# A prologue worked chunk by chunk, and a new order of all tasks, in a delta-rule attention with a routed expert layer

## The chip, the core and the metric

The kernel runs on one NeuronCore of a Trainium2 chip. The core has a matrix engine (TensorE, PE in the profile), a vector engine (VectorE, DVE), a scalar engine (ScalarE, ACT), a general engine (GpSimd, POOL) and a synchronising engine (SyncE, SP) which here only issues transfers. Each engine works through its own queue in order. Transfers between HBM and the on-chip memory SBUF are issued from the queues of SP, ACT and POOL, and the products of TensorE land in a separate memory, PSUM. The metric is the device time of one execution in microseconds (us), as the median of several runs.

## The reference

Two blocks follow one another. The first is a delta-rule attention over 4 batches of 8 heads, 768 steps and 48 features. With normalised keys, each step reads the state and then corrects it:

```python
for t in range(S):
    kt, vt, bt = (k_n[:, :, t], v[:, :, t], beta[:, :, t, None])
    y[:, :, t] = np.einsum('bhd,bhde->bhe', q[:, :, t], state)
    v_old = np.einsum('bhde,bhd->bhe', state, kt)
    state = state + bt[:, :, :, None] * np.einsum('bhd,bhe->bhde', kt, vt - v_old)
```

The second block takes the 3072 tokens of 384 features that come out. It chooses for each token one of 8 experts by the largest cosine with an expert's embedding, and computes `gate * (relu(x @ w1[e]) @ w2[e])` with that expert's weights (384x1024 and 1024x384). The gate is the softmax probability of the chosen expert.

## The kernel before

**Attention in chunks.** The 768 steps are cut into 12 chunks of `C = 64` steps (index m). Two batches and two heads stand side by side in the 128 rows of a tile. A chunk is worked in two *units* (n = 2m and 2m + 1, one for each pair of batches), so there are 24 units. Inside a chunk the steps are not taken one by one: the corrections of the 64 steps solve a triangular system, whose matrix comes from the products of the keys with one another, and the kernel forms inverses of its two 32x32 diagonal blocks once for each *group* g of two chunks (four units). There are 6 groups.

**From keys to inverses (`prepare(g)`).** For each chunk: load the keys k in eight transfers, two halves i with four each (`planned_k`, `load_swapped`, L283). Square them on ScalarE (L440), sum on VectorE (L445), take the root and its reciprocal and scale by the root of beta (L464, L389 to L391, L471, L479), and multiply the keys (L497). Turn them on TensorE (L298) and copy them out of PSUM on ScalarE into `KQ`. Multiply the keys with one another (`gram_keys`) and bring the diagonal blocks of both chunks into `stage`. One 128x1024 transpose on VectorE (L569) lays the blocks of all heads into lanes; POOL masks the upper part (`lower`, L574); and VectorE eliminates column by column, a product (L585 or L601) and a subtraction (L590 or L605) for each column.

**The first group is special.** For group 0 (`FINE`) the elimination runs only in two 16x16 blocks, columns 1 to 14 of 16, and TensorE finishes the 32x32 inverses: the row part goes back from the lanes (`rows_from_lanes`, L615) and is copied into `W` (`rows_spread`, two copies on ScalarE), then the rest (`from_lanes`, L620). Then come 64 small products (`level_one`), a copy to SBUF on ScalarE (`level_one_out`), 64 more products (`level_two`), a merge on VectorE (`merged`, L652) and two copies of the inverses into `W` on ScalarE (`spread`). A fp32 product stands in the trace as two records. The other groups eliminate all 30 columns on VectorE and have only the two copies at the end.

**A unit.** `gram` multiplies keys with keys and queries; `corner` (ScalarE, into `Sx`) and `scores` (VectorE, into `M`) mask the results. Then comes the chain: the product of state and keys (`old`), its subtraction from the scaled values V (`rest`, L758, into R), `solve` with W, copy Y, `fix`, copy U, `solve_again`, copy Z, `update`, and the new state on VectorE (L807; L809 in the first chunk). The first two units have no state, and begin with `solve`. `inside` and `from_state` give the unit's outputs, which go to the tokens' tile, are turned, and give the router's logits. `routing` works groups of four units: it writes tokens and lists of their numbers by expert to HBM (L1048, L1054).

**The order.** All of the attention stage is a list of tasks with dependencies (`plan.add`). The table `ORDER` gives the one order in which `Plan.emit` issues them. So each engine's queue is fixed by the table, and a task that waits holds up everything behind it on its engine. The numbers for busy time and due time in `plan.add` do not act at run time. Where two engines read one tile of PSUM, the second also waits for the first.

**Constants and loads.** `start_constants` fills zero columns on POOL, `masks` makes the masks on VectorE and fills `Sx` and `W` on POOL. Beta is loaded first on SP. Key halves go through SP, but the second half of chunk 0 through ScalarE's queue and that of chunk 1 through POOL's. `late_constants4` (L939 to L950) makes token numbers on VectorE.

**The experts.** Behind the plan, from L1312 on, tiles of up to 256 tokens are gathered and multiplied with the weights of their expert (L1278 and L1295). Weights of expert 0 are loaded into `w1_first` and `w2_first` during attention, in space that keys and inverses no longer use; two tiles of expert 0 are computed early.

## Time and profile before

| what | value |
|---|---|
| time, median of 3 runs | 603.27 us (599.58 to 604.70) |
| the profiled execution's own time | 605.27 us |
| its span, first to last instruction | 603.5 us |
| mean granted TensorE clock | 0.904 |
| TensorE busy | 520.3 us (86%) |
| VectorE busy | 275.3 us (46%) |
| ScalarE busy | 202.8 us (34%) |
| GpSimd busy | 171.9 us (28%) |
| first square of keys starts | 10.39 us |
| first solve of a unit starts | 74.60 us |
| first product of the experts' stage starts | 334.62 us |
| transfers | 90.49 MB |

A line of the timeline gives the start in us from the span's start, the length in us, the engine, the line of the code, the operation, and what it writes and reads ("out<-in") with the tile's size; "x2" means that neighbours are merged. Square brackets give the idle time ahead of it and what ended that. A line of windows gives the stretch and its length, the busy time of TensorE's products, its weight loads, VectorE, ScalarE and GpSimd (each with the number of instructions), the granted clock, the busy share of the transfer engines and GB/s. Names of tiles can be those of the space in which they lie: the keys lie in `w1_first`, and lanes and inverses in `w2_first`, which both read `w_first`.

### The profile page before, as it was taken

The page shows a single profiled execution, that of the slowest core. Times are in us where ns is not written, and L with a number is a line of the kernel's source. Part 1 is how long each engine was busy: PE and PEld are TensorE (multiplying, and loading weights), DVE is VectorE, ACT ScalarE, POOL GpSimd, SP SyncE. Part 2 cuts the span into 40 slices and gives each one's busy share as a digit, 9 for nine tenths or more (in the row PEclk, how much of TensorE's full clock was granted, in tenths as well). Part 3 has the DMA queues.
Part 4 walks back from the last instruction along what each step waited for, and adds up shares of the span by engine and source line. Part 5 has one row for each costly group of instructions (what it writes and reads, how often), then busy time and mean ns, then how long its engine had stood idle before and what let it go on. Part 6 is the DMA issues. An engine that isn't in the chain of part 4 may idle for free. (4 is left out here: it accounts for less than half of the span.)

```text
span 603.5 us, 20901 instructions
## 1 busy us (share of the span) xinstructions
PE 520.3 (86%) x9131; PEld 432.2 (72%) x9131; DVE 275.3 (46%) x756; ACT 202.8 (34%) x378; POOL 171.9 (28%) x230
## 2 busy tenths in 40 slices
PE   4478688987978986898899898999999999999990
PEld 3467587876867885787796777777776877777870
DVE  3796989988777868785315020110011221121100
ACT  2353368565555654437341111101101221110100
POOL 7321662155315305312414013411221111111000
PEclk9875589997697998768899899999999999999996
DMA  3434434355164430005502899997456756789300
GB/s 69 75 69 80 83 69 74 66 96 120 26 183 89 121 99 5 6 4 158 168 18 91 314 383 386 360 376 253 160 158 222 243 160 227 239 257 328 127 17 17
DMA packets 116330, 90.49 MB, mean 150 GB/s; under 512 B 83394, under 2 KB 105308, under 8 KB 116226
## 3 DMA queue, kind: packets, MB, share of 16 engines
q1 hardware_dynamic: 110722, 77.76, 43.8%
q0 software_dynamic: 4416, 11.06, 5.3%
q8 instruction: 76, 1.25, 0.8%
q10 hardware_dynamic: 1088, 0.20, 0.2%
q14 instruction: 28, 0.23, 0.1%
HBM read 77.06 MB, written 12.13 MB: 148 GB/s over the span
## 5 line engine op out<-in xcount | busy, mean ns | idle before, releaser
L1280 ACT ACTIVATE hT<-acc 128x512 f32<-128x512 f32 (+3 forms) x52 | 28.5, 548 | 168.5 <-PE acc L1278 168.4
L1278 PEld LDWEIGHTS acc<-xTm,w 128*128 128x128 f32 x576 | 77.7, 191 | 5.8 <-issue 1.8
L1278 PE MATMUL acc<-xTm,w 128*128 128x128 f32 (+3 forms) x576 | 80.3, 299 | 0.0
L1295 PE MATMUL acc<-w,hT 128*128 128x384 f32 (+2 forms) x272 | 78.9, 489 | 0.0
L1308 POOL DMA_INDIRECT out_dram<-y,more_ids x22 | 21.7, 987 | 160.9 <-DVE y L1298 128.3
L1295 PEld LDWEIGHTS acc<-w,hT 128*128 128x128 f32 (+2 forms) x272 | 42.2, 176 | 30.3 <-issue 5.8
L1269 DVE COPY xTm<-acc 128x384 f32<-128x384 f32 (+3 forms) x26 | 12.7, 509 | 105.6 <-PE acc L1268 104.8
L601 DVE TENSOR_TENSOR tmp<-w_first 128x30 f32<-128x30 f32 (+9 forms) x150 | 57.5, 383 | 4.9 <-POOL w_first L574 0.9
L605 DVE TENSOR_TENSOR w_first<-w_first,tmp 128x30 f32<-128x30 f32 (+9 forms) x150 | 55.9, 373 | 4.2
L1298 DVE TENSOR_SCALAR y<-acc,xg 128x384 f32<-128x384 f32 x20 | 12.4, 618 | 97.7 <-PE acc L1295 93.1
L262 PE MATMUL psum_pair<-KQ 48*64 48x64 f32 (+1 forms) x1536 | 41.4, 260 | 11.3 <-ACT KQ L265 8.2
L1278 PEld LDWEIGHTS acc<-xTm,w_first 128*128 128x128 f32 x288 | 43.7, 196 | 4.1 <-DVE xTm L1269 0.9
L1278 PE MATMUL acc<-xTm,w_first 128*128 128x128 f32 (+3 forms) x288 | 45.9, 321 | 0.8 <-DVE xTm L1269 0.8
L262 PEld LDWEIGHTS psum_pair<-KQ 48*64 48x64 f32 x1536 | 35.6, 156 | 14.7 <-ACT KQ L265 9.4
L1295 PE MATMUL acc<-w_first,hT 128*128 128x384 f32 (+2 forms) x176 | 44.2, 489 | 0.0
L262 PE MATMUL psum_pair<-S,KQ 48*64 48x64 f32 x1408 | 35.3, 247 | 9.1 <-ACT KQ L265 2.2
L262 PEld LDWEIGHTS psum_pair<-S,KQ 48*64 48x64 f32 x1408 | 30.3, 158 | 12.4 <-issue 3.0
L1054 POOL DMA_INDIRECT idmap<-tokid,slots_i x24 | 24.2, 1007 | 47.4 <-DVE tmp L601 20.6
L1295 PEld LDWEIGHTS acc<-w_first,hT 128*128 128x128 f32 (+2 forms) x176 | 23.1, 163 | 17.8 <-issue 4.5
L460 POOL TENSOR_TENSOR rt<-rn,half 128x32 f32<-128x32 f32 x4 | 21.9, 5483 | 32.4 <-DVE rn L445 32.4
L497 POOL TENSOR_TENSOR K<-w_first,rt 128x384 f32<-128x384 f32 x22 | 18.6, 865 | 36.7 <-PE psum_pair L262 18.3
L298 PE MATMUL psum_pair<-ident,K 128*128 128x128 f32 x96 | 18.2, 361 | 12.1 <-POOL space L915 7.1
(225 smaller groups left out, 840.3 us busy)
## 6 DMA issues: line engine op xcount, KB each, us to landing
w<-in_moe_w_dram SPq DMA_DIRECT2D x24, 1536.0 KB, 11.5
w_first<-in_moe_w_dram SPq DMA_DIRECT2D x10, 1536.0 KB, 8.4
q<-in_q_dram SPq DMA_DIRECT2D x96, 48.0 KB, 2.8
v<-in_v_dram SPq DMA_DIRECT2D x48, 96.0 KB, 2.7
w_first<-in_k_dram SPq DMA_DIRECT2D x88, 48.0 KB, 2.4
x_dram<-XC SPq DMA_DIRECT2D x5, 800.0 KB, 5.0
idmap<-space SPq DMA_DIRECT2D x1, 2048.0 KB
w_first<-in_moe_w_dram SPq DMA_DIRECT2D x6, 256.0 KB, 2.9
```

The lines of the kernel that those rows point to most:

```text
L262: nc.tensor.matmul(out_, lhsT=lhsT, rhs=rhs, start=start, stop=True, skip_group_check=True)
L298: nc.tensor.transpose(p[:, i, j * 128:(j + 1) * 128], two, ident)
L460: nc.gpsimd.tensor_tensor(out=flat(rt, part), in0=flat(ss, part), in1=half[:, 0:w], op=ALU.pow)
L497: (nc.vector if m == 1 else nc.gpsimd).tensor_tensor(heads(buf("K", m))[:, i], buf("k", m)[:, i], rt[:, m % 2, i].rearrange("p j jj -> p ( ...
L601: nc.vector.tensor_tensor(t, X[:, j + 1:, j:j + 1].broadcast_to([128, rows, j]), X[:, j:j + 1, 0:j].broadcast_to([128, rows, j]), op=ALU.mult)
L605: nc.vector.tensor_tensor(X[:, j + 1:, 0:j], X[:, j + 1:, 0:j], t, op=ALU.subtract)
L1054: put = nc.gpsimd.indirect_dma_start(out=idmap[:, :], out_offset=bass.IndirectOffsetOnAxis(ap=slot_i[:, i:i + 1], axis=0), in_=K["tokid"][ ...
L1269: nc.vector.tensor_copy(t.xT[:, :, b * T:b * T + n], psX[:, :, 0:n])
L1278: nc.tensor.matmul(psH[:, i, :], lhsT=t.w1[:, j, (f + i) * 128:(f + i + 1) * 128], rhs=t.xT[:, j, 0:t.width], start=(j == 0), stop=(j == K ...
L1280: nc.scalar.activation(t.hT[:, f:f + k, 0:t.width], psH, ACT.Relu)
L1295: nc.tensor.matmul(psO[c:c + w, :], lhsT=t.hT[:, f, b * T + o:b * T + o + w], rhs=t.w2[:, f, :], start=(f < q), stop=(f >= NF - q))
L1308: nc.gpsimd.indirect_dma_start(out=out[:, :], out_offset=bass.IndirectOffsetOnAxis(ap=t.ids[b][0:n, 1:2], axis=0), in_=y[0:n, :], in_offse ...
```

## The change

- **Loads.** The first halves of the keys of chunks 0 to 3 go through SP, the second halves through ScalarE's queue (16 transfers there instead of 4, none on POOL). The queries of chunk 0 (8 transfers) go through POOL's queue.
- **Masks.** `masks` keeps the six small column masks. The wide ones, the fine mask and POOL's fills go to a second task, `more_masks`.
- **Level products.** `level_one`, its copy, `level_two` and `merged` are each made for one chunk's heads (a = 0 or 1) at a time, in one bank of PSUM for each chunk, so that a step of one chunk waits only for that chunk's part. The merge is two instructions for each chunk.
- **Copies of the inverses.** For group 0 they are made for each chunk by itself, in two instructions each; the second block's copies (also that of the row part) are on VectorE instead of ScalarE. A unit reads only its own chunk's part of W.
- **Order.** `ORDER` has 1275 tasks instead of 1270 and is new throughout.

```diff
-            e, name, busy = (nc.sync, "SP", 2.2) if m > 1 or not i else (nc.scalar, "ACT", 2.8) if m == 0 else (nc.gpsimd, "POOL", 4.0)
+            e, name, busy = (nc.sync, "SP", 2.2) if m > 3 or not i else (nc.scalar, "ACT", 2.1)
...
+            plan.add("DVE", 2.0, 0.2, -39.0, more_masks, reads=["iotas", "masks"], writes=["masks2"])
...
                 def rows_spread(b=b, name=name):
-                    act_copy(W[:, :, b * HC:b * HC + LC], WN.rearrange("p r x -> p x r"), K[name])
+                    o, i_ = W[:, :, b * HC:b * HC + LC], WN.rearrange("p r x -> p x r")
+                    if b:
+                        nc.vector.tensor_scalar_mul(o, i_, K[name])
+                    else:
+                        act_copy(o, i_, K[name])
...
+            def level_one(a):
                 def step():
                     p = pair(level)
-                    for x in xs:
+                    for x_, x in enumerate(half_x[a]):
                         for o in range(2):
-                            mm(p[HALF[o], 0, x * LC:(x + 1) * LC], W[HALF[o], x], WT[HALF[o], LC:, x])
+                            mm(p[HALF[o], a, x_ * LC:(x_ + 1) * LC], W[HALF[o], x], WT[HALF[o], LC:, x])
...
+            def level_one_out(a):
+                to = WN.rearrange("p r x -> p (r x)")[:, a * HX:(a + 1) * HX]
+                return lambda: act_copy(to, pair(level)[:, a, 0:HX], K["lo"])
...
+            def merged(a):
+                def step():
+                    p = pair(level)[:, a, HX:2 * HX].rearrange("p (jj n c) -> p jj n c", jj=2, c=LC)
+                    for jj in range(2):
+                        to = WT.rearrange("p c (jj m n) -> p jj m n c", jj=2, m=2)[:, jj, a, :, LC:]
+                        nc.vector.scalar_tensor_tensor(out=to, in0=p[:, jj], scalar=K["lo"], in1=to, op0=ALU.mult, op1=ALU.add)
+                return step
...
+            if g == 0:
+                for a in range(2):
+                    def spread(b=b, name=name, a=a):
+                        for jj in range(2):
+                            x0 = jj * 16 + a * 8
+                            o, i_ = W[:, x0:x0 + 8, b * HC:(b + 1) * HC], WT.rearrange("p i x -> p x i")[:, x0:x0 + 8]
+                            if b:
+                                nc.vector.tensor_scalar_mul(o, i_, K[name])
+                            else:
+                                act_copy(o, i_, K[name])
...
-                load_swapped(nc.sync, by_head(heads(buf("q", m))), q, m, i)
+                load_swapped(nc.sync if m else nc.gpsimd, by_head(heads(buf("q", m))), q, m, i)
...
-        W_, S_ = [at("W", n // 4) + (0,), at("W", n // 4) + (1,)], ("S", i)
+        W_, S_ = [at("W", n // 4) + (b, m % 2) for b in range(2)], ("S", i)
```

## The prediction

> **What bounds the kernel now.** I read the page's slices first, then the timeline of the first 95 us, then the later timeline of VectorE, then windows with the granted clock. The slices show two stages: an attention stage, in which no engine is full, up to about 320 us, and an expert stage in which TensorE is full:
>
> ```profile
> PE   4478688987978986898899898999999999999990
> DVE  3796989988777868785315020110011221121100
> PEclk9875589997697998768899899999999999999996
> ```
>
> One slice is 15 us. From slice 22 on PE stands at 8 or 9, and the change touches no instruction there. So what the change is worth is how much earlier the experts' first product starts: 334.62 us in this trace.
>
> The head of the attention stage is a chain through one group of inverses. The timeline, columns start, length, instruction:
>
> ```profile
> 5.84 21.99 SPq L283 DMA_DIRECT2D w_first<-in_k_dram  x32
> 10.39 0.84 ACT L440 ACTIVATE sq<-w_first 128x768 f32<-128x768 f32 x1 [8.08 <-DMA w_first<-in_k_dram]
> 32.39 2.00 DVE L569 STREAM_TRANSPOSE w_first<-space 128x1024 f32<-128x1024 f32 x1
> 36.92 0.18 DVE L585 TENSOR_TENSOR tmp<-w_first 128x28 f32<-128x28 f32 x1
> ...
> 46.73 1.25 DVE L620 STREAM_TRANSPOSE w_first<-w_first 128x1024 f32<-128x1024 f32 x1
> 50.56 6.96 PE L262 MATMUL psum_pair<-w_first,W 64*64 64x16 f32 x128
> 58.37 7.01 PE L262 MATMUL psum_pair<-w_first,W 64*64 64x16 f32 x128 [0.44 <-ACT w_first L265]
> 69.33 1.13 DVE L652 SCALAR_TENSOR_TENSOR w_first<-psum_pair,lo,w_first 128x512 f32<-128x512 f32 x1
> 70.49 2.10 ACT L265 ACTIVATE W<-w_first,nfirst 128x1024 f32<-128x1024 f32 x1 [9.30 <-DVE w_first L652]
> 72.49 2.06 ACT L265 ACTIVATE W<-w_first,nsecond 128x1024 f32<-128x1024 f32 x1
> 74.60 1.99 PE L262 MATMUL psum_pair<-V,W 64*64 64x64 f32 x64 [1.62 <-ACT W L265]
> ```
>
> To be seen: the level products could start at 47.98, when the lanes are back, and start at 50.56 behind a gram product that waited for queries. They end at 65.38, but the merge comes at 69.33, because on VectorE it stands behind the next group's elimination. Then two copies follow one another on ScalarE. The first solve starts 26.6 us after the inverses' first form is there, and only 14 of them are level products.
>
> Behind the head, VectorE paces the next stretch (93.15 is the end of the second group's elimination, 106.83 the first subtraction of unit 4, 148.13 that of unit 8):
>
> ```profile
> 93.15 1.25 DVE L620 STREAM_TRANSPOSE w_first<-w_first 128x1024 f32<-128x1024 f32 x1
> 106.83 0.56 DVE L758 TENSOR_TENSOR R<-V,psum_pair 128x384 f32<-128x384 f32 x1 [0.56 <-PE psum_pair L262]
> 148.13 0.55 DVE L758 TENSOR_TENSOR R<-V,psum_pair 128x384 f32<-128x384 f32 x1
> ```
>
> In the windows of 10 us VectorE is busy 9.52, 8.96 and 9.46 from 95 to 125, but 6.61 to 8.79 from 145 to 175: there the chain of the units and TensorE's clock set the pace.
>
> **The change part by part,** by the order of the changed program on each queue and the durations above.
>
> *Loads.* A key load costs its queue 0.69 us (21.99/32 on SP; 2.74/4 on POOL; ScalarE the same). SP now starts with keys, so its half of chunk 0 is issued by 3.6. ScalarE issues 16 loads instead of 4, from 1.05 to 12.0, and the first square stands behind all of them: 12.0 instead of 10.39, a loss of 1.6. From there: square 0.84, sum 0.95, root 0.3, reciprocal and corrections 1.2 (14.76 to 15.92), second sum 0.95, beta's correction 0.95, the second chunk's scales 1.5, and some 0.8 of gaps between dependent instructions. Its keys' product starts at 19.5, against 19.61: the loss is made up, as chunk 1's keys also come sooner. On POOL the query loads (8 x 0.69) end at 14.3, ahead of the product for chunk 0, which needs its scale at 18: nothing. SP's loads for chunk 4 wait for that product (19.7, a ring of four), and behind them stand queries 1, chunk 5, values 0: these land by 34, 40 and 43 and are needed at 35, 45 and 59. Three queues at once I cannot read off this trace: one queue keeps the DMA engines 0.41 to 0.44 busy, two (6 to 8 us) 0.60. Bounds 0 and 2 us of loss; I take 0.5, as only 3 us have three queues. The values that now stand between key loads on SP cost 3 us of issue each and delay keys that have 10 us of slack by then.
>
> *Chunks 2 and 3, masks.* Both squares now precede the copies of the turned keys, which start at 22.95 instead of 24.49, as they no longer wait behind chunk 3's data and the large beta root. But the constants of 1.9 us (34.3 to 37.0 before, with a stall of 0.9) now stand ahead of the second roots on VectorE. Keys 2 and 3 start at 29.3: no change. The lane transpose comes at 31.5 instead of 32.39, elimination at 35.3 instead of 36.92, since no constants follow it. Splitting the masks adds nothing: VectorE waits from 6 to 11 us anyway.
>
> *Level products.* Elimination takes 7.7: 43.0. Transpose 1.04, VectorE's new copy of the row part (unseen there; a straight 128x512 takes 0.67, the strided merge 1.13: I take 0.9), memset 0.27, transpose 1.25: lanes back at 46.6. The gram products are done by 42.5, as query 1 now lands at 34; products start at 46.6. The copy between the levels stands on ScalarE behind a mask copy that waits for VectorE's scores (52.8, after the 2.0 transpose and six instructions); it runs at 53.3, when 7.0 us of first-level products have ended at 53.6. So no gap: 14.2 us, end 60.8 (before 65.38).
>
> Here a rule speaks. The Trainium skill (TensorE: Matmul & The Clock Gate, "Part 1: The HAM clock gate") says that about 3.4 us of sustained work lifts the clock from half to full. The trace disagrees for these products:
>
> ```profile
> 52.00:54.00 2.00, 2.00 (x42) 2.00 (x42) 1.00 (x3) 0.00 (x0) 0.33 (x2) 0.50 0.47 82
> 62.00:64.00 2.00, 2.00 (x42) 2.00 (x42) 1.79 (x9) 0.00 (x0) 2.00 (x1) 0.50 0.37 65
> ```
>
> TensorE is busy all of both windows, at 0.50. By the rule the unbroken 14 us would shrink by about 5; by the rows they stay. I take the rows.
>
> *Merge and copies.* The first half's merge needs 57.3 and VectorE: after its elimination steps, the scales (POOL's power ends at 55.6) and a sum it is free at 58.3. Two instructions of 0.3; then ScalarE's copy for chunk 0 in two parts of 0.6 (a quarter of 2.10 each, plus overhead) until 60.1, VectorE's until 60.5 (0.55 each, by the strided merge's 2.2 ns per element; straight would be 0.35). TensorE finishes level two at 60.8, then a transpose of keys 4 (1.9 at this clock) stands ahead: first solve 62.7, against 74.60. **11.9 us earlier.** A solve of chunk 0 reads only chunk 0's half, so the rest hides behind it.
>
> *What is late next.* VectorE now carries extra copies (0.9 and four of 0.55, 3.1 us) that ScalarE had. It loses the stall of 5.72 us at 53 to 58.7, but waits about 3.5 us for the first two states (69 to 71 and 74 to 75.7), because its order has fewer elimination steps ahead of them. From 64.3: 44 elimination instructions 17.2, other work 5.0, states 3.5, contention 1.0. The second group's inverse comes at 91.0 instead of 93.15: only 2 us gained. On ScalarE the copy of that inverse (2.1) now stands ahead of unit 2's last copy, so unit 2's state waits for it: 100 us, and unit 4's subtraction comes at 102.5 instead of 106.83, 4.3 earlier. Unit 5 follows at 105.3 (before 113.16). In the new order three states of units 4 to 6 stand before the third group's transpose (before, two), so unit 7's state comes at 139 (before 146.17), unit 8's subtraction at 139.5 instead of 148.13: **8.6 earlier.** From there each group holds the same instructions, and by the last group's transpose four state updates are left in both orders. I carry 8. Later on SP, the 2 MB fill of the token map (172.83 before) and the first expert's w1 stand earlier, and the list writes that wait for the fill (POOL idle 10.5 at 182) with them. POOL is 28% busy, and keys and values behind those writes wait for VectorE's scales anyway: nothing, with 3 us of delay for loads that the fill meets as the bad end.
>
> *Sum.* The profiled execution took 605.27 (span 603.5), 2.0 above the median of the three runs (603.27). 605.27 - 8 is 597.3; for the median, 603.27 - 8 = 595.3.
>
> **Rivals.**
> *A, the lead stays at 8 (0.48).* About 595; 589 to 599 with the loads' 2 us and 4 us of different queue order.
> *B, VectorE's pace swallows the lead (0.25).* For it: 9.5 of 10 busy from 95 to 125, and only 2 us gained at 91. Against: from 145 it has 20% idle, and the units run ahead of it in the new order. Then 2 us: 601.
> *C, slower: the clock in the body (0.19).* From 85 to 335 the granted clock lacks the equivalent of 59 us at half (twice the missing share of each 10 us window, summed), in runs such as 146 to 158 and 264 to 275, where TensorE is busy but slow. They follow thin stretches (1.84 busy of 4 at 134 to 138, 1.22 of 4 at 180 to 184). If the new order thins more, each us at half costs about half a us while the lead of 8 is spent: with 16 us more at half the lead is gone, from 28 on it is slower by over 1%. With 32 us more: 603 - 8 + 16, 611. Against it: the same engines, and shorter waits in the head.
> *D, all of the head (0.08).* Nothing swallows the 11.9, and the clock rises sooner: 590 or less, say 588.
> That the change doesn't do what it says can be left out for the halves: their instructions are in the program's order.
>
> **Numbers.** A measurement of this kernel tells about 1% (6 us) from none. Faster: 0.46 of A, D and a little of B: 0.55. Same: 0.26. Slower: 0.19, C. Range 584 to 609: from D to most of C. Predicted 595.3.
>
> **What would show it.** Level products starting near 46.6 without a gap, near 14 us at clock 0.5; merge at 58 to 61 in four parts; first solve near 63; second group's transpose near 91; unit 8's subtraction near 139.5; first expert product near 326.6. Wrong, if the first square comes after 14, if the first solve is later than 66, if the granted clock between 90 and 320 is more than 0.05 below that of before, or if ScalarE's copy of the second inverse holds units 2 and 3 past 104.

## The result, and the profile after

The change made the kernel a little slower, not faster: the median of 20 runs is 606.00 us (601.72 to 615.41) beside 602.28 us (596.88 to 610.33) for the kernel before in 20 runs on the same chip. The ratio is 1.0058, with a 95% interval of 1.0031 to 1.0085. The forecast of 595.3 us had the wrong sign; 606.0 lies in its range, and a change of 0.6% lies within the 1% that I had called no measurable change.

The profiled execution took 604.79 us (span 603.1, mean granted clock 0.911). That is 1.2 below its median, while that of before (605.27) lay 3.0 above the median here. The two traces are therefore equally long, and the loss of 3.7 us can't be read from their ends, only its causes from what lies between. In the comparisons below a ratio stands against the kernel before in its own group and leaves out disturbed runs, while a median is over all of a kernel's runs, and two groups (named there) were taken while every kernel, that of before included, took some 620 us.

The slices of the page after, 15 us each, show the two stages as before:

```profile
PE   0767978977797987897999998999999999999990
DVE  5799688877988779884215120110011121121100
PEclk9985599788997769789799998999999999999995
```

TensorE starts later: its first slice holds 0 where it held 4. The two slices with a clock of 5 (45 to 75 us) are the level products, as before. From slice 22 on PE stands at 8 or 9 in both pages.

The timeline of the head (start, length, instruction) holds the answer to most of the prediction's steps:

```profile
0.81 5.70 SPq L283 DMA_DIRECT2D w_first<-in_k_dram  x8
1.05 1.44 ACTq L283 DMA_DIRECT2D w_first<-in_k_dram  x2
2.52 11.02 ACTq L283 DMA_DIRECT2D w_first<-in_k_dram  x14
6.56 9.13 SPq L368 DMA_DIRECT2D XC<-in_beta_dram  x8
...
13.64 0.84 ACT L447 ACTIVATE sq<-w_first 128x768 f32<-128x768 f32 x1 [11.33 <-DMA w_first<-in_k_dram]
17.51 0.35 PE L262 MATMUL psum_pair<-ident,XC 8*64 8x8 f32 x2 [17.51 <-DMA XC<-in_beta_dram]
20.02 0.17 DVE L387 COPY beta_s<-psum_pair 128x16 f32<-128x16 f32 x1 [3.01 <-PE psum_pair L262]
24.76 1.02 DVE L504 TENSOR_TENSOR K<-w_first,rt 128x384 f32<-128x384 f32 x2
...
38.90 1.96 DVE L576 STREAM_TRANSPOSE w_first<-space 128x1024 f32<-128x1024 f32 x1
43.26 0.19 DVE L592 TENSOR_TENSOR tmp<-w_first 128x28 f32<-128x28 f32 x1
53.14 1.25 DVE L627 STREAM_TRANSPOSE w_first<-w_first 128x1024 f32<-128x1024 f32 x1
54.53 7.01 PE L262 MATMUL psum_pair<-w_first,W 64*64 64x16 f32 x128 [3.65 <-DVE w_first L627]
62.53 7.01 PE L262 MATMUL psum_pair<-w_first,W 64*64 64x16 f32 x128 [0.99 <-ACT w_first L265]
69.59 0.80 DVE L671 SCALAR_TENSOR_TENSOR w_first<-psum_pair,lo,w_first 128x128 f32<-128x128 f32 x2 [4.40 <-PE psum_pair L262]
71.55 2.21 PE L262 MATMUL psum_pair<-V,W 64*64 64x64 f32 x62
98.82 1.25 DVE L627 STREAM_TRANSPOSE w_first<-w_first 128x1024 f32<-128x1024 f32 x1
```

The loads of beta, its turning and the product for chunk 1 in the kernel before:

```profile
0.81 4.99 SPq L362 DMA_DIRECT2D XC<-in_beta_dram  x8
5.68 0.35 PE L262 MATMUL psum_pair<-ident,XC 8*64 8x8 f32 x2 [5.68 <-DMA XC<-in_beta_dram]
19.61 1.03 DVE L497 TENSOR_TENSOR K<-w_first,rt 128x384 f32<-128x384 f32 x2
```

Three things are to be seen. First, beta's eight loads now end at 15.69 (6.56 + 9.13), where they had ended at 5.80, and they took 9.13 us instead of 4.99. TensorE turns beta from 17.51 (5.68 before), VectorE waits 3.01 for it until 20.02, and the keys of chunk 1 are multiplied at 24.76 instead of 19.61. Second, from the start of the elimination to that of the level products there are 11.3 us, from there to the first solve 17.0: the head is shorter from the elimination on (28.3 instead of 37.7), but it starts 6.3 later. Third, the first solve comes at 71.55, only 3.05 earlier than before, and the inverse of the second group at 98.82, 5.67 later than before (93.15).

### The profile page after: what moved, and what is told of

Read it like the earlier page. It is cut to its first block, busy times and chain, and to the rows that moved or that the text cites. A ratio compares the mean times of both kernels' runs of the same rounds, so it can differ in the third digit from the quotient of the medians.

```text
span 603.1 us, 20921 instructions
## 1 busy us (share of the span) xinstructions
PE 517.2 (86%) x9131; PEld 430.1 (71%) x9131; DVE 280.8 (47%) x766; ACT 200.2 (33%) x380; POOL 172.9 (29%) x234
## 5 line engine op out<-in xcount | busy, mean ns | idle before, releaser
L1330 PE MATMUL acc<-w,hT 128*128 128x384 f32 (+2 forms) x272 | 80.4, 494 | 0.0
L608 DVE TENSOR_TENSOR tmp<-w_first 128x30 f32<-128x30 f32 (+9 forms) x150 | 56.0, 373 | 4.4 <-POOL w_first L581 0.3
L262 PE MATMUL psum_pair<-KQ 48*64 48x96 f32 (+1 forms) x1536 | 43.2, 265 | 8.7 <-DVE S L842 4.6
L1313 PEld LDWEIGHTS acc<-xTm,w_first 128*128 128x128 f32 x288 | 42.2, 191 | 4.0 <-DVE xTm L1304 0.8
L1313 PE MATMUL acc<-xTm,w_first 128*128 128x128 f32 (+3 forms) x288 | 44.5, 314 | 0.7 <-DVE xTm L1304 0.7
L262 PE MATMUL psum_pair<-S,KQ 48*64 48x64 f32 x1408 | 33.6, 241 | 8.0 <-DVE S L842 4.5
L262 PEld LDWEIGHTS psum_pair<-S,KQ 48*64 48x64 f32 x1408 | 28.9, 153 | 11.2 <-DVE S L842 4.7
L265 ACT ACTIVATE KQ<-psum_pair 128x1024 f32<-128x1024 f32 x24 | 24.5, 1022 | 11.6 <-PE psum_pair L298 11.4
L1286 POOL DMA_INDIRECT xg<-x_dram,more_ids x23 | 22.5, 977 | 19.6 <-DMA more_ids<-idmap 7.7
```

What stands on the lines that cost most here:

```text
L262: nc.tensor.matmul(out_, lhsT=lhsT, rhs=rhs, start=start, stop=True, skip_group_check=True)
L265: nc.scalar.activation(out_, in_, ACT.Copy, scale=scale)
L608: nc.vector.tensor_tensor(t, X[:, j + 1:, j:j + 1].broadcast_to([128, rows, j]), X[:, j:j + 1, 0:j].broadcast_to([128, rows, j]), op=ALU.mult)
L1286: t.read = nc.gpsimd.indirect_dma_start(out=t.x[b], out_offset=None, in_=x_dram[:, :], in_offset=bass.IndirectOffsetOnAxis(ap=t.ids[b][:, ...
L1313: nc.tensor.matmul(psH[:, i, :], lhsT=t.w1[:, j, (f + i) * 128:(f + i + 1) * 128], rhs=t.xT[:, j, 0:t.width], start=(j == 0), stop=(j == K ...
L1330: nc.tensor.matmul(psO[c:c + w, :], lhsT=t.hT[:, f, b * T + o:b * T + o + w], rhs=t.w2[:, f, :], start=(f < q), stop=(f >= NF - q))
```

## The experiments

**Are the loads the loss?** Letters in the expectations stand for theories, which each text explains. My theory after the trace was that they are, by way of beta. The rival was that the new order itself costs the time, in ScalarE's copies or in the clock. The first group of runs changes the loads alone, in both kernels.

Beta ahead of the keys on SP, all else as changed (task 5 is beta's load):

```diff
-0 1 3 106 2 4 108 15 6 5 8 7
+0 5 1 3 106 2 4 108 15 6 8 7
...
```

> The changed kernel, with one edit: the eight loads of beta stand first on SP instead of behind eight key loads. In the changed kernel's trace VectorE waits for beta from 16.98 to 20.02 us; with beta first that wait of 3.0 goes, while the keys of chunk 0 still land by 13.6 us (ScalarE's 16 loads set the first square). Expected: first elimination step near 40.3 instead of 43.26, first solve near 68.5 instead of 71.55. Theory H (a lead at the first solve is carried to the end at its size): 3 us faster than the changed kernel, ratio to before 1.001. Theory P (VectorE's pace and the order of the body swallow a lead): within 1 us of the changed kernel, ratio 1.005 to 1.007.

Measured: 607.64 us, ratio 1.0039 (1.0015 to 1.0063). Beta was not quicker where it stood first:

```profile
0.81 11.03 SPq L368 DMA_DIRECT2D XC<-in_beta_dram  x8
...
12.06 11.68 SPq L283 DMA_DIRECT2D w_first<-in_k_dram  x16
16.78 0.84 ACT L447 ACTIVATE sq<-w_first 128x768 f32<-128x768 f32 x1 [14.47 <-DMA w_first<-in_k_dram]
```

While ScalarE's queue issues keys, eight loads of beta hold SP for 11 us, and SP's keys start only at 12.06. The elimination starts at 43.9 (43.3 in the changed kernel). So not the place of beta on SP was wrong, but that it shares the time with ScalarE's key loads.

The loads of before in the changed kernel, with the queries of chunk 0 left on POOL:

```diff
-e, name, busy = (nc.sync, "SP", 2.2) if m > 3 or not i else (nc.scalar, "ACT", 2.1)
+e, name, busy = (nc.sync, "SP", 2.2) if m > 1 or not i else (nc.scalar, "ACT", 2.8) if m == 0 else (nc.gpsimd, "POOL", 4.0)
...
-0 1 3 106 2 4 108 15 6 5 8 7
+5 1 3 105 108 106 107 0 4 2 15 6 8 7
...
```

> The changed kernel with the load order of the kernel before: beta first on SP, second key halves of chunk 0 on ScalarE's queue, of chunk 1 on GpSimd's, of chunks 2 and 3 on SP; chunk 0's queries stay on GpSimd's queue. Expected: first square near 10.4 us as before, first elimination step near 37 (43.26 in the changed kernel), first solve near 65.3 (71.55). H: 6 us faster than the changed kernel, ratio to before 0.996. P: within 1.5 us of the changed kernel, ratio 1.004 to 1.006.

Measured: 602.03 us, ratio 0.9965 (0.9935 to 0.9994), against 607.64 for the one above in the same group. The elimination starts at 39.0, the first solve comes at 67.3, the second inverse at 93.1, unit 8's subtraction at 151.5. That is the time that H expected (0.996).

A third set of loads has beta on POOL's queue ahead of its fills, and eight key loads on ScalarE ahead of its table load:

```diff
-nc.sync.dma_start(out=bt[32 * jj + i * NP:32 * jj + (i + 1) * NP, :, o], in_=b[jj])
+nc.gpsimd.dma_start(out=bt[32 * jj + i * NP:32 * jj + (i + 1) * NP, :, o], in_=b[jj])
...
```

> The changed kernel with its loads arranged for the first square: beta from GpSimd's queue ahead of its fills, first key halves of chunks 0 and 1 on SP, second ones ahead of the table load on ScalarE's queue, chunks 2 and 3 whole on SP. Expected: first square near 7.5 us, first elimination step near 36 (the second roots then wait for VectorE's own work), first solve near 63 to 64, against 71.55. H: 7 to 8 us faster than the changed kernel, ratio to before 0.993 to 0.995. P: within 1.5 us of the changed kernel, ratio 1.004 to 1.006.

Measured: 603.04 us, ratio 0.9967 (0.9932 to 1.0002). The first square came at 9.25, but the masks came late: the number patterns they are made of stood behind beta on POOL, so the first sum followed only at 15.2. The elimination started at 40.8. The time is that of the old loads all the same, though the second inverse came 2.0 us later (95.2) and H had expected 0.993 to 0.995.

The reverse, the new loads in the kernel before:

```diff
-e, name, busy = (nc.sync, "SP", 2.2) if m > 1 or not i else (nc.scalar, "ACT", 2.8) if m == 0 else (nc.gpsimd, "POOL", 4.0)
+e, name, busy = (nc.sync, "SP", 2.2) if m > 3 or not i else (nc.scalar, "ACT", 2.1)
...
-load_swapped(nc.sync, by_head(heads(buf("q", m))), q, m, i)
+load_swapped(nc.sync if m else nc.gpsimd, by_head(heads(buf("q", m))), q, m, i)
```

> The kernel before with the loads of the change alone: 16 second halves from ScalarE's queue, beta behind eight key loads on SP, chunk 0's queries from GpSimd's queue; all the rest as before. Expected: first square near 13.6 instead of 10.39, keys' product of chunk 1 near 24.8 instead of 19.61, first elimination step near 43 instead of 36.92, first solve near 80.5 instead of 74.60. H: 6 us slower than before, ratio 1.010. P: the lag is made up by the middle of the attention stage, ratio 1.000 to 1.003.

(The places of the load tasks in the table go with it.) Measured: 609.92 us (six runs), ratio 1.0115 (1.0068 to 1.0161). Here, too, beta took 9.23 us, and keys 1 were multiplied at 25.1. So the loads alone cost the kernel before about 1%, and the changed kernel with old loads stands at 0.9965 where with its own it stood at 1.0058. That they cost time is shown from both sides. How much of it is beta's lateness and how much that of the first square is read from the trace only: no run takes beta away from ScalarE's key loads and leaves those as they are.

**What are the split and the order worth?** The change's code with the loads and the order of before, and the order without the code (both taken at the level of 620 us; the kernel before 623.08 beside them):

```diff
-load_swapped(nc.sync if m else nc.gpsimd, by_head(heads(buf("q", m))), q, m, i)
+load_swapped(nc.sync, by_head(heads(buf("q", m))), q, m, i)
...
-0 1 3 106 2 4 108 15 6 5 8 7
+5 1 3 105 108 106 107 0 8 4 2 15
...
```

> The code of the change (split masks, level products, merges and copies for each chunk, second block's copies on VectorE) with the loads and the task order of the kernel before; each new part stands where its whole stood. The merge still stands behind the second group's elimination steps on VectorE (69.33 before), so the first solve should come near 71.5 instead of 74.60, and VectorE carries some 2.2 us of copies more ahead of the second group's transpose (93.15). Theory D (VectorE's queue decides; an earlier first solve alone is swallowed): +0 to +2 us, ratio 1.000 to 1.004. Theory C (the chain from the first solve decides): 3 us faster, ratio 0.995.

> The code of the kernel before with its key and beta loads, but the relative order of the changed kernel for all other tasks (chunk 0's queries on GpSimd's queue, as that order needs them early); level products, merge and copies of the inverses unsplit, each at the place of its last part. First elimination step near 39 as in the run with the old loads, first solve near 70 (67.3 there). D: the order of the body is what the run with the old loads gained, so near it: ratio 0.996 to 1.000. C: 2.5 to 3 us slower than that run: ratio 1.001.

Measured: the split alone 621.77 us, 0.9962 (0.9918 to 1.0006); the order alone 631.41 us, 1.0161 (1.0097 to 1.0224), with a mean granted clock of 0.880 against 0.897 of the kernel before. For the split alone D had expected 1.000 to 1.004 and C 0.995: the time is C's, but the second inverse, too, came earlier than before (91.7 for 93.15), which D had not expected, so the run does not separate the two. For the order alone neither theory had room for a loss of 1.6%. A third kernel of that group had the old loads and a leaner head: the corrections of later betas and the constants stand behind the first elimination on VectorE.

```diff
...
-110 13 111 109 303 112 30 34 27 31 503 113 114
+110 13 111 109 30 34 27 112 31 113 35 32 114
...
```

> The run with the old loads, with its head reordered: on VectorE the first group's transpose and elimination stand ahead of the token constants and of the beta corrections for groups 2 to 5, which move behind the elimination and into the wait ahead of the merge; on ScalarE the copies of the turned keys stand ahead of chunk 3's square; on TensorE the first level stands ahead of the score products of units 1 and 2. First elimination step near 33 instead of 39.0, first solve near 60 instead of 67.3, second group's inverse back near 88 to 90 instead of 93.1. D and C both: 3 to 6 us faster than the run with the old loads, ratio to before 0.987 to 0.992. If a lead in the head is swallowed whatever moves it: ratio 0.995 to 0.998, as with the old loads.

Measured: 629.19 us, 1.0133 (1.0098 to 1.0169). Its elimination did start at 32.8, but beside POOL's product of the keys its first instructions took 0.75 to 0.83 us instead of 0.2, and the second inverse came at 95.3. It lost, where all theories had expected a gain, with a clock of 0.886. So at this level both kernels with the new order lost over 1%.

At the ordinary level (the kernel before 603.08) I ran three of these again: the changed kernel, with the old loads, and the split alone.

> The changed kernel itself, on the same chip as the three runs beside it. Before, on its own chip: ratio 1.006. If the order of the body costs granted clock on some chips (the order's runs showed 0.880 and 0.886 where the kernel before had 0.897), ratio up to 1.02 with a clock some 0.01 below that of before; if only its loads cost time, 1.006.

> The changed kernel with the loads of the kernel before, as in the run a_old_loads (ratio 0.9965 there), on the same chip as the changed kernel: the loads' cost in the new order by itself. By the head's lag of 4 to 6 us: 0.7 to 1.0% faster than the changed kernel, whatever the chip.

> The run split_only once more (code of the change, loads and order of the kernel before), on the same chip as the changed kernel with old loads: the two differ in the order alone. If the new order is worth its lead of 3.4 us at the first solve: that run is 3 us faster than this one. If the order gains nothing behind the head: the same within 1.5 us, both near 0.996. If it costs granted clock: this one is faster, and shows the higher clock.

Measured: 604.62 us, 1.0047 (1.0010 to 1.0084); 601.23 us, 1.0009 (0.9981 to 1.0037); 602.10 us, 0.9966 (0.9935 to 0.9997). The loads again make a difference of 3.4 us between the first two, though their intervals overlap. Between the second and the third there is none that these runs tell: the order on top of the split brings nothing clear.

**Does the first solve set the end, or VectorE's queue?** The prediction carried the lead of the first solve to the end. If that is right, a kernel that only brings the first solves forward gains. The split alone, with the level products' copies and the chains of units 0 and 1 moved up in the table:

```diff
-134 135 136 137 138 139 140 141 142 143 92 144
+134 135 136 137 138 74 77 75 81 139 140 141
...
```

> The run split_only (code of the change, loads and order of before) with the chain of the first two units moved up and VectorE's amount of work untouched: the merges stand right behind the level products on VectorE, the scaling of values 0 ahead of the roots on GpSimd (idle there for 7.9 us), and solve to update of units 0 and 1 ahead of the turning of keys 4 and 5 on TensorE and ScalarE. First solve near 62.5 instead of 70.7 us; the copies of the first states keep their place in VectorE's queue (near 80 to 82). Theory D (VectorE's queue decides): the lead of 8 us is swallowed, within 1.5 us of split_only. Theory C (the chain from the first solve decides): 6 to 8 us faster than split_only, ratio to before near 0.985.

Measured: 607.51 us (six runs), 1.0116 (1.0058 to 1.0174), 1.5% slower than the split alone, where D had expected at most 1.5 us and C a gain.

```profile
63.38 0.76 DVE L671 SCALAR_TENSOR_TENSOR w_first<-psum_pair,lo,w_first 128x128 f32<-128x128 f32 x2 [3.13 <-PE psum_pair L262]
...
64.71 2.92 PE L262 MATMUL psum_pair<-V,W 64*64 64x64 f32 x64 [1.38 <-ACT W L265]
94.35 1.25 DVE L627 STREAM_TRANSPOSE w_first<-w_first 128x1024 f32<-128x1024 f32 x1
```

The first solve came 7.1 us earlier than in the split alone (71.80), but VectorE now waits 3.13 us for the merge, since fewer elimination steps stand ahead of it; the second inverse comes at 94.35 instead of 92.65, unit 8's subtraction at 151.6 instead of 147.9. The experts' first product comes at 334.78 instead of 329.71. So the lead of the first solve was worth nothing. The wait on VectorE is one cause that fits the loss; it is not shown to be the only one, for the granted clock was lower too: 0.899 in the mean of these runs, 0.914 in the kernel before and 0.915 in the split alone beside them.

The counterpart leaves the first solve and puts idle work on VectorE, 26 copies of 128x64 that nobody reads, behind the copies of the first inverses:

```diff
+                        if a and b:
+                            for _ in range(26):
+                                nc.vector.tensor_copy(K["col_f"], K["trow_f"])
```

> The run split_only (ratio 0.9962 and 0.9966) with 26 idle copies of 128x64 on VectorE right behind the copies of the first inverses: some 5 us more of VectorE's time behind the merges and ahead of the second group's inverse. First solve unchanged near 71.3, second group's inverse near 97.7 instead of 91.7 to 92.7. Theory D (the time of the second group's inverse on VectorE decides): 4 to 5 us slower than split_only, ratio 1.004 to 1.006. Theory C (the first solve decides): within 1.5 us of split_only, ratio 0.996 to 0.999.

Measured: 611.27 us, 1.0108 (1.0079 to 1.0138). The idle copies and the second inverse, and below them the second inverse of the split alone:

```profile
69.89 5.92 DVE L696 COPY col_f<-trow_f 128x64 f32<-128x64 f32 x26
97.04 1.25 DVE L627 STREAM_TRANSPOSE w_first<-w_first 128x1024 f32<-128x1024 f32 x1
...
92.65 1.25 DVE L627 STREAM_TRANSPOSE w_first<-w_first 128x1024 f32<-128x1024 f32 x1
```

The copies took 5.92 us, the second inverse came 4.4 later, and the first solve at 70.36, a little earlier. So more work on VectorE alone makes the kernel slower, which is the sign that this theory expected. The size is larger: some 8.6 us against the split alone (1.0108 less 0.9966, times 605). The two traces show where it arises: 5.3 us stand at unit 8's subtraction (153.20 for 147.89) and 12.0 at the experts' first product (341.74 for 329.71). In between the clock differs, 0.83 from 150 to 330 us instead of 0.88. Summed as in the prediction, from 85 to 345 us it lacks 68.8 us at half instead of 54.4; at half a us each the difference is, as an estimate, 7 us. Whether the idle work lowers the clock or it was lower by chance, one trace of each can't tell; the mean of the runs was 0.904, and 0.911 in the kernel before beside them.

Put together, for kernels in the old order: with the second inverse at 91.7 and 92.7 the ratio was 0.9962 and 0.9966, at 94.3, 95.8 and 97.0 it was 1.0116, 1.0115 and 1.0108. The first solves of the same five (70.7, 71.8, 64.7, 77.8, 70.4) don't sort them. The kernel before itself fits in between (93.15 and 1), but two versions that follow below don't give the sizes: one at 95.0 has 1.0019, and one at 88.2 no better than 0.9941. So the second inverse sorts the kernels of this order roughly, and the two experiments that delay it had a lower clock as well.

**A version that beats both.** If the second inverse counts, the split in the old order should gain with quicker loads and less on VectorE. A first try put beta on ScalarE's queue, all keys on SP but for chunk 1's second half, the second block's copies on ScalarE, and constants into VectorE's wait for the merge:

```diff
-nc.sync.dma_start(out=bt[32 * jj + i * NP:32 * jj + (i + 1) * NP, :, o], in_=b[jj])
+nc.scalar.dma_start(out=bt[32 * jj + i * NP:32 * jj + (i + 1) * NP, :, o], in_=b[jj])
...
-                            if b:
-                                nc.vector.tensor_scalar_mul(o, i_, K[name])
-                            else:
-                                act_copy(o, i_, K[name])
+                            act_copy(o, i_, K[name])
```

> The run split_only with VectorE's queue shortened ahead of the second group's inverse: beta from ScalarE's queue and chunk 0's keys whole on SP (first square near 8.4 instead of 10.3 us), the token constants from ahead of the first elimination into VectorE's wait behind the second group's first product (3.5 us there), and the second block's copies of the inverses on ScalarE again. First elimination step near 34 instead of 37, first solve near 69 to 70 instead of 71, second group's inverse near 88 instead of 92. D: 4 us faster than split_only, ratio 0.989 to 0.991. C: 1.5 us faster, ratio 0.994.

Measured: 605.96 us, 1.0019 (0.9982 to 1.0056), with the second inverse at 95.0. It missed the forecast by the loads, once more beta beside keys, now with the queues exchanged:

```profile
0.81 16.56 ACTq L368 DMA_DIRECT2D XC<-in_beta_dram  x8
...
18.81 0.83 ACT L447 ACTIVATE sq<-w_first 128x768 f32<-128x768 f32 x1
```

The second try has beta on POOL's queue, behind the number patterns and ahead of the fills, the second half of chunk 0 on ScalarE ahead of its table load, and all other keys on SP. The changed kernel got the same loads and nothing else (the lines show the edit against it):

```diff
-nc.sync.dma_start(out=bt[32 * jj + i * NP:32 * jj + (i + 1) * NP, :, o], in_=b[jj])
+nc.gpsimd.dma_start(out=bt[32 * jj + i * NP:32 * jj + (i + 1) * NP, :, o], in_=b[jj])
...
-e, name, busy = (nc.sync, "SP", 2.2) if m > 3 or not i else (nc.scalar, "ACT", 2.1)
+e, name, busy = (nc.scalar, "ACT", 2.1) if m == 0 and i else (nc.sync, "SP", 2.2)
...
```

> The run split_best with other loads: beta from GpSimd's queue right behind its number patterns and ahead of its fills, chunk 0's second key half ahead of the table load on ScalarE's queue, all other keys on SP from the start. Token constants in VectorE's wait and second block's copies on ScalarE as there. In the runs so far eight beta loads took 5.0 us from GpSimd's queue whatever the others did, but 9 to 17 us beside key loads on SP or ScalarE. First square near 6 us (10.3), keys' product of chunk 1 near 16 (19.6), first elimination step near 32 (37), second group's inverse near 87 (92.7). D: 5 to 6 us faster than split_only, ratio 0.987 to 0.990. If the head's loads are no longer what sets VectorE's queue there: ratio 0.993 to 0.996.

> The changed kernel with the loads of split_pool_beta and nothing else (chunk 0's queries stay on GpSimd's queue, behind beta and the fills). First square near 6 us instead of 13.6, keys' product of chunk 1 near 16 to 17 instead of 24.8, first elimination step near 36 instead of 43.3, second group's inverse near 91 instead of 98.8. D: 7 us faster than the changed kernel (1.0058 and 1.0047), ratio 0.993 to 0.995. If the loads are not what the change lost by: 1.003 or more.

Measured, at the level of 620 us (the kernel before 624.63): 617.79 us, 0.9939 (0.9894 to 0.9984), and 629.96 us (six runs), 1.0182 (1.0126 to 1.0237) at a clock of 0.881 beside 0.900. Once more a kernel with the new order lost at this level. All of it again at the ordinary level (the kernel before 603.28), with the changed kernel beside them:

> The run new_pool_beta once more, side by side with the changed kernel. In its first run everything, the kernel before too (625 us), was slower than in the other runs (603), and every kernel with the new order lost 1.3 to 1.8% there. If the loads are what the change loses by: 1.0% faster than the changed kernel beside it (6 us, its second inverse 6 us earlier), and at a time near 603 of before a ratio of 0.994 to 0.998. If the new order itself loses: the same as the changed kernel within 0.3%.

> The changed kernel itself beside new_pool_beta2. Where the kernel before takes near 603: ratio 1.004 to 1.006. Where it takes near 620: by the runs with the new order there, 1.02 to 1.03, with a granted clock 0.015 to 0.02 below that of before.

> The run split_pool_beta (0.9939) once more, in the same company. D: its second inverse 4 us ahead of split_only's gives 0.989 to 0.993 where before takes near 603; at least 1.2% faster than the changed kernel in either case.

Measured: the changed kernel with these loads 0.9938 (0.9902 to 0.9973), the changed kernel 605.47 us and 1.0011 (0.9979 to 1.0043; after 1.0058 and 1.0047, so it gained in no group and lost clearly in two), the split with these loads 599.50 us and 0.9941 (0.9913 to 0.9969). For the first, take the ratio with care: its 22 times lie in two heaps, 594.7 to 602.1 and 605.0 to 609.6 us, and the median of all is 603.50. The last is the best of all versions, and it held at both levels. Its head:

```profile
0.81 23.76 SPq L283 DMA_DIRECT2D w_first<-in_k_dram  x34
0.82 2.71 ACTq L283 DMA_DIRECT2D w_first<-in_k_dram  x4
1.76 4.98 POOL L363 DMA_DIRECT2D XC<-in_beta_dram  x8
8.69 0.84 ACT L447 ACTIVATE sq<-w_first 128x768 f32<-128x768 f32 x1 [3.64 <-DMA w_first<-in_k_dram]
...
17.77 1.03 DVE L504 TENSOR_TENSOR K<-w_first,rt 128x384 f32<-128x384 f32 x2
33.73 0.20 DVE L592 TENSOR_TENSOR tmp<-w_first 128x28 f32<-128x28 f32 x1 [1.37 <-POOL w_first L581]
```

Beta takes 4.98 us on POOL's queue, with SP and ScalarE issuing beside it; the elimination starts 9.5 us earlier than in the changed kernel, and the second inverse comes at 88.2. By D that should have brought 0.989 to 0.993 and 1.2% over the changed kernel; it brought 0.7%. Against the split alone, whose second inverse came 4.4 us later, it brought about 0.25% (0.9941 beside 0.9966), some 1.5 us. So D's size failed here on the other side.

## Why the prediction was wrong, step by step

**Loads, the step that failed.** "Its keys' product starts at 19.5": it started at 24.76. Two terms were wrong. A key load on ScalarE's queue took 0.79 us (11.02/14), not the 0.69 of the trace before, so the first square came at 13.64, not 12.0. The larger one is beta: the step followed keys, queries and values through the queues and gave beta's own eight loads, now behind SP's keys, no time at all. It had bounded three queues at once by "0 and 2 us of loss; I take 0.5". Beta's loads took 1.14 us each instead of 0.62 and ended 9.9 later. Five microseconds at the keys' product were the price, outside of both bounds, and with the 2.7 us of the next step they use up the lead of 8. The loads account for the sign and not for all that was missing: with them mended the changed kernel reached 0.9965, 1.0009, 0.9967 and 0.9938, at best 3.7 us faster than before, not 8. The prediction had named a first square after 14 as a sign of error. The square stayed below that; the sign that mattered, beta's copy on VectorE, was not on its list, while the one further on, a first solve later than 66, did show.

**Chunks 2 and 3, masks.** Predicted 35.3 for the elimination, measured 43.26. Of the 8.0, 5.3 come from the keys' product. The other 2.7 lie on VectorE: 2.1 had gathered by the transpose (38.90 for 31.5), and 0.6 came between it and the elimination. On both sides of the transpose VectorE corrects later betas, some of them at three to five times their usual 0.21 us:

```profile
36.71 0.70 DVE L396 SCALAR_TENSOR_TENSOR quot<-quot,beta_s 128x48 f32<-128x48 f32 x1
37.45 0.76 DVE L397 SCALAR_TENSOR_TENSOR sqb<-sqb,quot 128x48 f32<-128x48 f32 x1
...
40.78 0.41 DVE L395 RECIPROCAL quot<-sqb 128x48 f32<-128x48 f32 x1
41.22 1.02 DVE L396 SCALAR_TENSOR_TENSOR quot<-quot,beta_s 128x48 f32<-128x48 f32 x1
42.27 0.21 DVE L397 SCALAR_TENSOR_TENSOR sqb<-sqb,quot 128x48 f32<-128x48 f32 x1
42.40 0.94 DVE L452 TENSOR_REDUCE rn<-sq 128x16 f32<-128x768 f32 x1
```

**Elimination and lanes: right.** 7.83 for 7.7, and 11.3 us from the elimination to the level products, as worked out.

**Level products: right on the clock, wrong on the halves.** The windows of the changed kernel, in the columns explained above, show TensorE busy in all of both at half clock, so the decision for the rows and against the rule held:

```profile
55.00:57.00 2.00, 2.00 (x43) 2.00 (x42) 2.00 (x2) 0.00 (x0) 0.45 (x1) 0.50 0.36 68
64.00:66.00 2.00, 2.00 (x42) 2.00 (x40) 1.16 (x4) 0.00 (x0) 1.68 (x3) 0.50 0.41 81
```

But there is a gap of 0.99 between the levels (predicted none), and "the first half's merge needs 57.3" fell: it started at 69.59, after 4.40 us of waiting for TensorE, 0.05 after the last of all 128 products. In `ORDER` the products of both chunks stand ahead of either chunk's copy and merge, and in no run did a copy or a merge start before all the products of its level were through (in the early version, too, the merge came at 63.38, at the end of level two at 63.33). I had ruled out "doesn't do what it says" for the halves; on the chip the splitting of the merge decoupled nothing. What I had overlooked is in the program itself: as built, the first merge waits for TensorE's counter to stand at 424, which the last product of chunk 1 sets, while those of chunk 0 set 392; and the first product of level two waits for both copies (31 on ScalarE's counter, which only the second copy sets). So the description of the change, by which a step of one chunk waits only for that chunk's part, does not hold for these waits. Whether another place in `ORDER` would give earlier waits no run tells. It did not cost the first solve anything against the sum, for the sum, too, let TensorE finish first: 62.7 + 8.0 + 1.0 is 71.7, measured 71.55.

**Copies and the first solve.** The 11.9 us became 3.05 because of the head's 8.0 and the gap's 1.0. From the first solve to the second inverse I had 28.3; it was 27.3. So that part of the sum was right, and 98.82 instead of 91.0 is the head again.

**What is late next.** Unit 4's subtraction was predicted at 102.5 and came at 112.72. With the loads mended it came at 105.4, unit 5's at 108.3 (predicted 105.3): near the sum. But unit 8 came at 156.05 (mended: 150.9), not at 139.5. The step "three states of units 4 to 6 stand before the third group's transpose" overlooked ScalarE between them:

```profile
115.55 0.55 DVE L793 TENSOR_TENSOR R<-V,psum_pair 128x384 f32<-128x384 f32 x1
...
126.48 0.49 ACT L265 ACTIVATE Y<-psum_pair 128x384 f32<-128x384 f32 x1
138.38 0.56 DVE L842 TENSOR_TENSOR S<-S,psum_pair 128x384 f32<-128x384 f32 x1 [3.45 <-PE psum_pair L262]
```

From unit 5's subtraction to the copy Y of its solve there are 10.9 us (4.3 before, from 113.16 to 117.42). Of these, 4.7 lie on TensorE, whose clock stood at 0.50 to 0.55 from 114 to 120 (the solve ends at 120.25), and 6.2 on ScalarE, where the copy now stands behind squares, turned keys and key blocks. The state that follows holds VectorE for 3.45 us, and the third inverse comes at 145.5 instead of 130.7. But 2.06 of the 3.45 are a pause of TensorE, in which it waits for nothing that the profile shows ("issue"), while the transfer engines are full:

```profile
134.00:136.00 2.00, 0.35 (x25) 0.27 (x14) 0.86 (x5) 0.00 (x0) 0.00 (x0) 1.00 1.01 370
...
136.41 0.28 PE L262 MATMUL psum_pair<-U,W 64*64 64x64 f32 x4 [2.06 <-issue]
```

The fill of the token map, issued at 130.09, falls here; in the kernel before it was issued at 172.83, and a pause of 2.07 us ended at 183.58, far behind the third inverse. The prediction had put the earlier fill at nothing, with a delay for loads alone. That the fill makes the pause is not tested, and since the table also puts more ahead of that inverse, I don't put all of its delay down to the copy and the pause.

**The body.** "From there each group holds the same instructions. I carry 8" failed to the other side. From unit 8 to unit 23 the changed kernel takes 140.7 us (156.05 to 296.73), the kernel before 150.7 (148.13 to 298.78; the split alone, in a quicker trace and nearly the same order as before, 144.9). A deficit of 7.9 at unit 8 is a lead of 2.1 at unit 23 and of 2.2 at the experts' first product (332.46 beside 334.62). Two errors thus cancelled in the trace, which was luck, and its lead did not come out in the median. The lines, the last two from the kernel before:

```profile
156.05 0.55 DVE L793 TENSOR_TENSOR R<-V,psum_pair 128x384 f32<-128x384 f32 x1
296.73 0.56 DVE L793 TENSOR_TENSOR R<-V,psum_pair 128x384 f32<-128x384 f32 x1 [0.78 <-PE psum_pair L262]
332.46 6.79 PE L1313 MATMUL acc<-xTm,w_first 128*128 128x160 f32 x48 [0.67 <-DVE xTm L1304]
...
298.78 0.56 DVE L758 TENSOR_TENSOR R<-V,psum_pair 128x384 f32<-128x384 f32 x1 [1.37 <-PE psum_pair L262]
334.62 8.18 PE L1278 MATMUL acc<-xTm,w_first 128*128 128x160 f32 x48 [0.84 <-DVE xTm L1269]
```

**The rivals.** The ordinary clock was not the cause: summed as in the prediction, the granted clock from 85 to 345 lacks 58.0 us at half in the changed kernel and 61.2 in that of before. So rival C, the only one on the slower side, had the sign but not the mechanism. Rival B's 2 us is what the trace shows at the experts. A slower head, by its loads, was a rival that I didn't have.

**What stays open.** At the 620 us level the three kernels with the new order that ran there lost 1.3 to 1.8% with granted clocks of 0.880 to 0.886, where the kernel before had 0.897 to 0.900, while the split in the old order kept its gain. Whether the clock is the cause there or goes along with it I can't tell; the changed kernel itself was not run at that level. The traces narrow it down: the experts' stage takes 268 to 274 us in all twenty of them, so all differences arise ahead of it, and from 85 to 345 us the clock lacks 88 to 106 us at half in these three, 72 in the split alone there, and 54 to 72 at the ordinary level. Also open is what the second inverse is worth by itself, as every kernel that delays it differs in loads or in clock too. The trace's lead of 2.2 us at the experts and the median's loss of 3.7 don't contradict one another: 4.2 of the 5.9 us between them are the places of the two traced executions beside their medians (3.0 above, 1.2 below), and 1.7 lie in the experts' stage of these two traces (270.6 us, and 268.9 before).

## What to carry to other kernels

When loads move between queues, list every load of the queues concerned with its new start, the small ones too, and find the first reader of each: here eight small loads set the head, and the large ones that the change was about did not. A duration of an issue holds only for the queues that were issuing beside it in that trace; a bound for another mix should be a multiple of the row, not a microsecond. And before a lead is carried to the end, ask what the steps behind it wait for: here a first solve 7 us earlier was worth nothing, and the second inverse on VectorE told the kernels apart better, though not by its size.

## What the runs showed of the hardware

**Issue times depend on who else issues.** Eight loads of beta took 4.99 us on SP with few loads beside them, 4.97 on POOL's queue with SP and ScalarE issuing, but 9.13, 9.23 and 11.03 on SP beside ScalarE's key loads, and 16.56 on ScalarE's queue beside SP's keys. In the three runs on SP, GpSimd issued eight query loads as well (8.57 to 13.77); which neighbour counts is not separated. Key loads suffered far less (0.69 to 0.88 each). The Trainium skill (DMA: Bandwidth & Descriptors, "Issuing engines are not separate DMA queues") says that issuing from several engines saves only the time to issue; in these runs that time itself doubled and tripled for the small loads on the queues of SP and ScalarE, and not on that of POOL. Why is not shown.

**VectorE stalls beside GpSimd.** VectorE's two mask instructions of 128x64 took 6.09 and 6.03 us and ended at 8.72, just as POOL's fills ended (8.64); before, they took 2.85 and 2.73 and ended at 4.46, where the first run of POOL's fills ended (4.38). In the lines above, a correction with two tensors in SBUF took 0.70 to 1.02 us beside POOL's work and 0.21 otherwise, while reciprocals with one input kept 0.41 to 0.44. The Trainium skill (GPSIMD Engine Reference, "1. Specifications") names contention with VectorE's instructions that have two inputs in SBUF or run in a two-port mode. For the corrections, which have two inputs, the rows agree, and the measured size is up to eight times the instruction (1.69 us for 0.21 at 27.42, beside a product of POOL from 27.43 on). The mask instructions have one input each; whether they run in such a mode no row here shows.
